# Block-sparse attention over gathered keys and values, and a feed-forward part without GpSimd, on one core

## The chip, the core and the metric

The kernel runs on one NeuronCore of a Trainium2 chip. The core has five engines that run at the same time, each with its own queue of instructions in a fixed order: TensorE (PE, matrix products; its weight loads are listed apart as PEld), VectorE (DVE), ScalarE (ACT), GpSimd (POOL) and SyncE (SP, which here only issues transfers). Engines wait for each other through semaphores. Data lie in SBUF, 128 partitions wide; matrix products land in PSUM, which has eight banks a partition; transfers between DRAM and SBUF, and within SBUF, are carried by 16 DMA engines. The metric is the device time of one execution in microseconds, the median of several.

## What is computed

Attention first, for 4 batches, 8 heads, 768 places and 64 numbers a head; then a feed-forward layer over the 3072 tokens with 512 inputs and 2048 hidden units.

```python
mask = np.abs(blk_i - blk_j) <= 1                       # blocks of 32 places, 24 of them
mask = mask | (blk_i == 0) | (blk_j == 0) | (blk_i == 23) | (blk_j == 23)
for qb in range(24):
    for kb in sampled_blocks[qb]:                       # three random blocks, the same for all heads
        mask[qb*32:(qb+1)*32, kb*32:(kb+1)*32] = True
attn = softmax(where(mask, q @ k.T / 8, -1e9))          # 1e-9 is added to the sum
x = (attn @ v), heads side by side                      # 3072 x 512
h = x @ w_in                                            # 3072 x 2048, weights given in float64
g = h * erf(log(1 + exp(h)))
out = g @ w_out                                         # 3072 x 512
```

So a query block in the middle (1 to 22) sees at most eight key blocks: its own and its two neighbours, blocks 0 and 23, and three random ones, some of which may coincide. Query blocks 0 and 23 see all 768 places.

## The kernel before

Attention goes head by head. A query tile has 128 queries of one head, and its scores are taken against all 768 keys, masked ones too. The mask is part of the product: 32 extra rows hold, for each query, a large negative number for each key block it must not see, and for each key the unit vector of its block (`mask_rows`, `spread`). In the first batch the product is taken in plain float32, four TensorE instructions a tile; later in two products of a rounded float32 and its remainder (`prep_head`, which also splits each head's values into a high and a low float16 half, L328 and L329). TensorE's line is L344.

A tile's softmax is: the row maximum (VectorE, L346), its scaling (L348), the exponential with the row sum (ScalarE, L350), a float16 copy (L356 on ScalarE or L358 on VectorE), the remainder in float16 (L360, mostly GpSimd), and one transposing transfer of both halves by SyncE (L362). Four tiles later `values` multiplies the transposed probabilities by the values: twelve products of 128 or 64 columns (L379, L380), and the quotient (L387 to L397). When a pair of heads is done, its outputs are split and transposed for the feed-forward part (L403 to L406).

The weights arrive as float64 bits, 32 pieces of 512 columns. VectorE takes each apart in three integer passes (L210 to L212); after the largest entry is known, each is scaled and split into two float16 halves in place (L290 to L297).

The feed-forward part works on 256 tokens and two hidden tiles of 128 at a time, a group of 512 columns; there are 96 groups. The first product has 24 matmuls of 256 columns (L460 to L462). Six passes of ScalarE (L464 to L475) and five of VectorE follow (L466, L473, L474, L476, L478), then the remainder of the float16 halves (L480), on GpSimd in three batches and on VectorE in the last. Three groups later the second product takes 12 matmuls of 512 columns (L492 to L494), in two halves.

The order of the work is set by a loop over query tiles: after each tile some steps of the weights and, with a credit for each batch, halves of feed-forward groups are issued. A planner places the instructions in the queues of the engines by a model of their times.

Of the kernel before, what the change touches and what calls it, by code (L numbers as in the profile page):

```python
# [10 lines left out]
F32R = mybir.dt.float32r  # L11
# [4 lines left out]
PSUM = bass.MemoryType.PSUM  # L16

P = 128
BLOCK = 32
NEG_BIG = float(2**33)  # /8 it exceeds the reference's 1e9  # L20
# [9 lines left out]
def sparse_attention_moe(ctx: ExitStack, tc: tile.TileContext, qT, kT, v, sampled, w_in, w_out, out):  # L30
    nc = tc.nc
# [4 lines left out]
    NQ = S // P  # query tiles, and key tiles, of a head  # L36
    NK = DM // P  # contraction tiles of the first product
    NF = DFF // P  # hidden tiles
    NR = sampled.shape[1]
    HB = min(512, S)  # L40
# [11 lines left out]
    st = ctx.enter_context(tc.tile_pool(name="st", bufs=4))  # L52
# [8 lines left out]
    # each batch's query tiles in two parts, head by head, so that the feed-forward part follows early  # L61
    hsegs = [(b, h, tuple(ts)) for b in range(B) for ts in (range(4), range(4, NQ)) for h in range(H)]
    raws = {}
    MR = slice(D, D + BLOCK)
    NATIVE = 2 * H  # parts of heads whose scores are taken in float32 as it is, while TensorE has time

    def stacked(n):
        """Places for two consecutive heads' queries and keys with the mask rows below them."""
        dt = F32 if n < NATIVE else F32R
        return [  # L70
            tuple(
                at.tile([D + BLOCK, S], dt, tag=f"{c}2", name=f"{c}2_{n}_{i}") for c in "qk"
            )
            for i in range(2)
        ]

    qk2 = {0: stacked(0)}

    def qk2_of(n):
        return qk2[0 if n < NATIVE else NATIVE][n % 2]  # L80

    def load_head(n):
        b, h, ts = hsegs[n]
        if n < NATIVE:
            q2, k2 = qk2_of(n)
            nc.sync.dma_start(q2[:D, : len(ts) * P], qT[b, h][:, ts[0] * P : (ts[-1] + 1) * P])
            nc.sync.dma_start(k2[:D], kT[b, h])
            return
        qraw = ld.tile([D, S], F32, tag="qraw", name=f"qraw_{n}", bufs=1)
        kraw = ld.tile([2 * D, S], F32, tag="kraw", name=f"kraw_{n}", bufs=1)  # L90
        nc.sync.dma_start(qraw[:, : len(ts) * P], qT[b, h][:, ts[0] * P : (ts[-1] + 1) * P])
        nc.sync.dma_start(kraw[:D], kT[b, h])
        nc.sync.dma_start(kraw[D:], kT[b, h])
        raws[b, h, ts] = (qraw, kraw)
# [3 lines left out]
    def load_v(b, h):  # L98
        vr = ld.tile([P, NQ, D], F32, tag="vraw", name=f"vraw_{b}_{h}", bufs=H)
        nc.sync.dma_start(vr, v[b][:, h])  # L100
        vraws[b, h] = vr

    load_head(0)

# [1 line left out]
    def pow2_scale(bound, tag, squared):  # L106
        """2^13 / 2^r and its inverse, on every partition, with 2^(r+1) above the largest entry
        of `bound`, or above its root."""
# [8 lines left out]
        zero = 63 if squared else 127  # what e is for r = 0  # L117
# [6 lines left out]

    vscale = {}

    vmax = {}

    def max_v(b, h):
        if b not in vmax:  # L130
            vmax[b] = st.tile([P, H], F32, tag="vmax", name=f"vmax_{b}", bufs=2)
        nc.vector.reduce_max(
            vmax[b][:, h : h + 1], vraws[b, h].rearrange("p k d -> p (k d)"), AX.X, apply_absolute_value=True
        )

    def scale_v(b):
        vscale[b] = pow2_scale(vmax.pop(b), f"v{b}", False)

# [1 line left out]

    unit = cp.tile([BLOCK, NB], F32, tag="unit", name="unit")
    nc.gpsimd.memset(unit, 1.0)
    nc.gpsimd.affine_select(unit, unit, [[1, NB]], ALU.is_equal, 0.0, base=0, channel_multiplier=-1)
    samp = at.tile([BLOCK, NB, NR, 2], I32, tag="pf", name="samp", bufs=3)
    nc.sync.dma_start(samp, sampled.bitcast(I32).rearrange("i (r w) -> i r w", w=2).partition_broadcast(BLOCK))
    hits = at.tile([BLOCK, 2, NB, NR], F32, tag="pf", name="hits", bufs=3)
    sampf, hit = hits[:, 0], hits[:, 1]
    nc.vector.tensor_copy(sampf, samp[:, :, :, 0])
    pidx = cp.tile([BLOCK, 1], F32, tag="pidx", name="pidx")
    nc.gpsimd.iota(pidx, [[0, 1]], base=0, channel_multiplier=1, allow_small_or_imprecise_dtypes=True)  # L150
    nc.vector.tensor_scalar(hit, sampf, pidx, None, ALU.is_equal)
    allow = cp.tile([BLOCK, NB], F32, tag="allow", name="allow")
    nc.vector.reduce_max(allow, hit, AX.X)
    # window |i-j| <= 1, key blocks 0 and NB-1, query blocks 0 and NB-1
    fixed = cp.tile([BLOCK, NB], F32, tag="fixed", name="fixed")
    nc.gpsimd.memset(fixed, 1.0)
    nc.gpsimd.affine_select(fixed, fixed, [[1, NB]], ALU.is_ge, 0.0, base=1, channel_multiplier=-1)
    nc.gpsimd.affine_select(fixed, fixed, [[-1, NB]], ALU.is_ge, 0.0, base=1, channel_multiplier=1)
    nc.gpsimd.affine_select(fixed, fixed, [[0, NB]], ALU.not_equal, 1.0, base=0, channel_multiplier=1)
    nc.gpsimd.affine_select(fixed, fixed, [[0, NB]], ALU.not_equal, 1.0, base=-(NB - 1), channel_multiplier=1)  # L160
    nc.gpsimd.memset(fixed[:, 0:1], 1.0)
    nc.gpsimd.memset(fixed[:, NB - 1 : NB], 1.0)
    nc.vector.tensor_tensor(allow, allow, fixed, ALU.max)
    bias = cp.tile([BLOCK, NB], F32, tag="bias", name="bias")
    nc.vector.tensor_scalar(bias, allow, -1.0, NEG_BIG, ALU.add, ALU.mult)

    def spread(rows, blocks):
        n = blocks.shape[1]
        nc.vector.tensor_copy(
            rows[MR, : n * BLOCK].rearrange("p (n c) -> p n c", c=BLOCK),  # L170
            blocks.unsqueeze(2).to_broadcast([BLOCK, n, BLOCK]),
        )

    masked = {}

    def mask_rows(n, ts):
        q2, k2 = qk2_of(n)
        key = (n >= NATIVE, n % 2)
        if key not in masked:
            spread(k2, unit)  # L180
# [410 lines left out]
```

## Time and profile before

| what | value |
|---|---|
| time, median of 3 runs | 1172.63 us (1172.04 to 1173.95) |
| span of the profiled execution | 1170.1 us; its own time outside the span is not listed, the median is 2.5 us above it |
| TensorE busy, mean granted clock | 910.7 us (78%), 0.876 |
| VectorE busy | 1045.3 us (89%) |
| ScalarE busy | 721.9 us (62%) |
| GpSimd busy | 662.0 us (57%) |
| moved by the DMA engines | 140.71 MB |

The page gives busy time by engine, a row of 40 slices, the chain of work that ended last, and groups of instructions. In a group's line stand the line of the kernel, the engine, the operation, what it writes and reads, shapes and count; behind the bar the busy time and the mean duration of one in ns; behind the second bar how long the engine was idle just before such instructions and what ended the wait. A TensorE instruction's duration includes the way through the array, so the distance between starts tells its rate. The granted clock is the share of full speed that TensorE was given.

### The profile page before, as it was taken

To read this page: it belongs to the slowest core of one execution; us is meant where nothing else is said; L and a number is where in the kernel's file an instruction comes from. 1 tells how busy PE (TensorE), PEld (TensorE's weight loads), DVE (VectorE), ACT (ScalarE), POOL (GpSimd) and SP (SyncE) were. 2 spreads that over 40 slices of the span, in tenths; PEclk is the share of its full clock that TensorE was granted. 3 is DMA by queue.
4 is the path that set the end of the run, shared out by engine and by line. 5 is a ranking of instruction groups with operands and counts; after the bars stand their busy time and mean duration, and the time that the engine had idled before them with its cause. 6 is when DMAs were issued, how large, how long until landed. Compare 5 with 4: busy or idle time off the path is not lost.

```text
span 1170.1 us, 18635 instructions
## 1 busy us (share of the span) xinstructions
PE 910.7 (78%) x6528; PEld 609.4 (52%) x6528; DVE 1045.3 (89%) x1672; ACT 721.9 (62%) x1389; POOL 662.0 (57%) x426
## 2 busy tenths in 40 slices
PE   4766666876888887776888888866988788889998
PEld 2433434543555654553665565544656555556664
DVE  6979976995999999996999999997998989997765
ACT  3557565763665766664666666654666765576775
POOL 1336674773767677685777667755666666741000
PEclk7566776897989989997988899897998989899999
DMA  9785966661665566763674567653744555451000
GB/s 331 137 240 125 216 128 138 129 118 34 133 131 115 115 147 137 138 141 72 121 157 98 115 129 165 127 130 75 132 99 101 122 111 119 96 93 34 20 18 19
DMA packets 354270, 140.71 MB, mean 120 GB/s; under 512 B 330976, under 2 KB 337152, under 8 KB 354176
## 3 DMA queue, kind: packets, MB, share of 16 engines
q1 hardware_dynamic: 350720, 133.23, 53.8%
q10 hardware_dynamic: 3456, 6.29, 1.6%
q8 instruction: 51, 0.84, 0.3%
q14 instruction: 43, 0.35, 0.1%
HBM read 51.40 MB, written 6.29 MB: 49 GB/s over the span
## 4 chain that ended last, share of the span: by engine, by line
DVE 58%; issue 13%; PE 10%; ACT 7%; DMA 3%; POOL 1%; SPq 0%; ACTq 0%; DVEq 0%; POOLq 0%
DVE mx L346 9%; DVE p L358 6%; DVE hs L476 6%; DVE x L466 5%; DVE s L474 5%; DVE s L473 4%; DVE vhl L329 4%; DVE g L478 2%; DVE q L321 2%; ACT pf L350 2%; DVE xf L397 2%; DMA pT<-p 2%; PE h L460 1%; PE h L461 1%; PE h L462 1%
## 5 line engine op out<-in xcount | busy, mean ns | idle before, releaser
L360 POOL TENSOR_TENSOR p<-pf,p 128x768 f16<-128x768 f32 x174 | 321.4, 1850 | 198.6 <-DVE p L358 62.5
L344 PE MATMUL s<-k,q 96*128 96x512 f32 (+3 forms) x768 | 265.4, 476 | 123.6 <-ACT pf L350 112.9
L350 ACT ACTIVATE pf<-s,nb 128x768 f32<-128x768 f32 x192 | 171.8, 895 | 147.1 <-DVE nb L348 119.7
L344 PEld LDWEIGHTS s<-k,q 96*128 96x128 f32 (+1 forms) x768 | 147.7, 225 | 203.7 <-ACT pf L350 129.5
L460 PE MATMUL h<-xT,wi 128*128 128x256 f16 x768 | 217.8, 284 | 14.5 <-DMA xT<-x 8.3
L462 PE MATMUL h<-xT,wi 128*128 128x256 f16 x768 | 216.9, 282 | 3.8 <-POOL wi L297 3.8
L461 PE MATMUL h<-xT,wi 128*128 128x256 f16 x768 | 217.4, 283 | 0.0
L379 PE MATMUL po<-vhl,pT 128*128 128x128 f16 x1152 | 143.7, 239 | 81.2 <-DVE y L392 41.0
L346 DVE TENSOR_REDUCE mx<-s 128x1 f32<-128x768 f32 x192 | 180.8, 943 | 6.8 <-PE s L344 6.7
L379 PEld LDWEIGHTS <-pT 128*128 128x128 f16 x1152 | 116.7, 110 | 112.8 <-issue 77.9
L494 PE MATMUL o<-wo,g 128*128 128x512 f16 x384 | 148.5, 396 | 21.8 <-POOL g L480 21.8
L492 PE MATMUL o<-wo,g 128*128 128x512 f16 x384 | 154.5, 402 | 10.5 <-DVE g L478 8.9
L493 PE MATMUL o<-wo,g 128*128 128x512 f16 x384 | 153.7, 400 | 0.0
L480 POOL TENSOR_TENSOR g<-hs,g 128x512 f16<-128x512 f32 x72 | 99.5, 1382 | 68.9 <-DVE g L478 53.8
L380 PE MATMUL po<-vhl,pT 128*128 128x64 f16 x1152 | 137.6, 209 | 0.0
L380 PEld LDWEIGHTS <-pT 128*128 128x128 f16 x1152 | 112.7, 106 | 12.3 <-issue 10.0
L475 ACT ACTIVATE s<-s 128x512 f32<-128x512 f32 x96 | 60.3, 628 | 93.2 <-DVE s L474 92.8
L474 DVE SCALAR_TENSOR_TENSOR s<-s,s 128x512 f32<-128x512 f32 x96 | 102.4, 1066 | 14.5 <-ACT s L472 13.6
L324 POOL TENSOR_TENSOR k<-kraw,k 64x768 fp32r<-64x768 f32 x48 | 103.4, 2154 | 18.5 <-DVE k L320 7.6
L467 ACT ACTIVATE x<-x 128x512 f32<-128x512 f32 x96 | 60.2, 627 | 86.8 <-DVE x L466 86.6
L358 DVE CAST p<-pf 128x768 f16<-128x768 f32 x124 | 104.0, 839 | 10.3 <-ACT pf L350 5.4
L476 DVE SCALAR_TENSOR_TENSOR hs<-s,hs 128x512 f32<-128x512 f32 x96 | 99.7, 1039 | 14.3 <-ACT s L475 14.1
(104 smaller groups left out, 1676.9 us busy)
## 6 DMA issues: line engine op xcount, KB each, us to landing
kraw<-in_kT_dram SPq DMA_DIRECT2D x96, 192.0 KB, 3.3
vraw<-in_v_dram SPq DMA_DIRECT2D x32, 192.0 KB, 2.8
wo<-in_w_out_dram SPq DMA_DIRECT2D x10, 512.0 KB, 5.1
wi<-in_w_in_dram SPq DMA_DIRECT2D x8, 512.0 KB, 6.1
wo<-in_w_in_dram SPq DMA_DIRECT2D x8, 512.0 KB, 9.3
k<-in_kT_dram SPq DMA_DIRECT2D x16, 192.0 KB, 3.3
pT<-p SPq DMA_TRANSPOSE x192, 3.7
qraw<-in_qT_dram SPq DMA_DIRECT2D x24, 128.0 KB, 3.0
```

The lines of the kernel that those rows point to most:

```text
L344: nc.tensor.matmul(s[:, c:e], lhs[:, qs], rhs[:, c:e], start=i == 0, stop=i == len(passes) - 1)
L346: nc.vector.reduce_max(mx, s[:, :S], AX.X)
L350: nc.scalar.activation(pf, s[:, :S], AF.Exp, bias=nb, scale=1.0 / math.sqrt(D), accum_out=sums[:, j : j + 1])
L358: nc.vector.tensor_copy(p2[:, 0], pf)
L360: eng.tensor_tensor(p2[:, 1], pf, p2[:, 0], ALU.subtract)
L379: nc.tensor.matmul(po[:, u, :], pT[:, k, :], vhl[:, k, :], start=k == 0, stop=False)
L380: nc.tensor.matmul(po[:, u, :D], pT[:, NQ + k, :], vhl[:, k, :D], start=False, stop=k == NQ - 1)
L460: nc.tensor.matmul(hj, hi, xa, start=kt == 0, stop=False)
L461: nc.tensor.matmul(hj, hi, xb, start=False, stop=False)
L462: nc.tensor.matmul(hj, lo, xa, start=False, stop=kt == NK - 1)
L474: nc.vector.scalar_tensor_tensor(s2, s1, C3, s2, ALU.add, ALU.mult)
L476: nc.vector.scalar_tensor_tensor(hs, s2, -1.0, hs, ALU.add, ALU.mult)
```

## The change

Attention no longer computes masked scores. The query blocks 1 to 20 of a batch form five tiles of four blocks; one unit is such a tile for four heads, 128 queries by 4 x 256 keys in two banks. For a block the 256 key places are: its own and two neighbouring blocks, read where they lie; three random blocks, copied within SBUF to a small buffer (`gather`), each by a SyncE transfer whose source is given by a register that SyncE reads from `sampled`; and blocks 0 and 23. There are six such buffers. Each block, head and piece is a product of its own, on an array of 64 rows and 32 columns, all in plain float32. Blocks 21 and 22 form a unit "e" for each four heads, and blocks 0 and 23, which see everything, a unit "f" for each two.

Values are split once for each batch and written to a table in DRAM with 32 rows of zeros at its end; a column of ones beside them gives the sums. GpSimd gathers the 256 rows of a block with two indirect transfers from a list of row numbers (`indices`, `gather_v`); a random block that coincides with another one is sent to the zero rows, so that it adds nothing to values or sums. The value products have 128 rows and 32 columns of the array and 64 or 65 streamed columns, four blocks in turn.

The weights are scaled and split in two passes instead of three, none on GpSimd. In the feed-forward part the remainder is always VectorE's; the second product follows two groups later instead of three. The feed-forward part may start when two query tiles of all heads are done, so a batch is released in three parts; it does not start before all weights are split. A quarter of the softmax remainders and the copies that reorder keys by blocks stay on GpSimd.

```diff
-NATIVE = 2 * H  # parts of heads whose scores are taken in float32 as it is, while TensorE has time
-    FF_LAG = 3  # groups between the two products
-    PV_LAG = 4  # query tiles between scores and values
+    KGS, VGS = 6, 8
+    FF_LAG = 2
+    PV_LAG = 2
...
+    def gather(b, i):
+        kg = at.tile([P, NR, HP, BLOCK], F32, tag="kg", name=f"kg_{b}_{i}", bufs=KGS)
+        for r in range(NR):
+            (load,), (n,) = nc.values_load_multi_w_load_instructions(
+                samp[0:1, i, r, 0:1], [mybir.EngineType.SP], min_val=0, max_val=NB - 1, ...)
+            tc.keep_in_program_order(load)
+            nc.sync.dma_start(
+                kg[:, r].rearrange("p a c -> p (a c)"),
+                kxs[b].rearrange("p n a c -> p n (a c)")[:, bass.ds(n, 1), :].rearrange("p n c -> p (n c)"),
+            )
...
+    def gather_v(b, quad, i):
+        vg = at.tile([P, 2, QW], F16, tag="vg", name=f"vg_{b}_{quad}_{i}", bufs=VGS)
+        if i < 0:
+            nc.sync.dma_start(vg, rows[:, -2 * i - 2 : -2 * i])
+        else:
+            for half in range(2):
+                nc.gpsimd.indirect_dma_start(out=vg[:, half], out_offset=None, in_=vtab[b, quad],
+                    in_offset=bass.IndirectOffsetOnAxis(ap=idx[:, half, i - 1 : i], axis=0))
...
-                if i % 2:
-                    nc.vector.tensor_scalar(w32, w32, s, None, ALU.mult)
-                else:
-                    nc.scalar.activation(w32, w32, AF.Copy, scale=s)
-                if i % 4:
-                    nc.scalar.activation(hi16, w32, AF.Copy)
-                else:
-                    nc.vector.tensor_copy(hi16, w32)
-                nc.gpsimd.tensor_tensor(lo16, w32, hi16, ALU.subtract)
+                nc.scalar.activation(hi16, w32, AF.Copy, scale=s)
+                nc.vector.scalar_tensor_tensor(lo16, w32, s, hi16, ALU.mult, ALU.subtract)
...
+    def softmax(s, groups, width, tag, u, place="pT"):
+        nc.vector.reduce_max(mx, s.rearrange("p (g w) -> p g w", w=width), AX.X)
+        nc.vector.tensor_scalar(nb, mx, -1.0 / math.sqrt(D), P_SHIFT * math.log(2.0), ALU.mult, ALU.add)
+        for g in range(groups):
+            nc.scalar.activation(pf[:, c], s[:, c], AF.Exp, bias=nb[:, g : g + 1], scale=1.0 / math.sqrt(D))
+        nc.scalar.activation(p3[:, :, 0], pf3, AF.Copy)
+        eng = nc.gpsimd if pick(u, 0.25) else nc.vector
+        eng.tensor_tensor(p3[:, :, 1], pf3, p3[:, :, 0], ALU.subtract)
+        nc.sync.dma_start_transpose(out=pT, in_=p2)
...
+    def key_columns(b, i, rows, pr):
+        return (
+            (0, 96, kx[rows, i - 1 : i + 2, pr, :]),
+            (96, 192, kg[rows, :, pr, :]),
+            (192, 256, kx[rows, 0 : NB : NB - 1, pr, :]),
+        )
...
+            for r in range(2):
+                pr = 2 * quad + r
+                for j in range(4):
+                    for a in range(2):
+                        rows, o = slice(a * D, a * D + D), slice(j * 32, j * 32 + 32)
+                        for c, e, keys in key_columns(b, 1 + 4 * t + j, rows, pr):
+                            nc.tensor.matmul(s4[o, a, r, c:e], qt[rows, pr, o], keys, start=True, stop=True)
...
+            for m in range(max(len(x) for x in todo)):
+                for j in range(4):
+                    if m < len(todo[j]):
+                        lhs, rhs = todo[j][m]
+                        nc.tensor.matmul(
+                            po[j * 32 : j * 32 + 32, hl, :w], lhs, rhs, start=m == 0, stop=m == len(todo[j]) - 1
+                        )
...
-        eng = nc.vector if b == B - 1 else nc.gpsimd
-        eng.tensor_tensor(g[:, 1], hs, g[:, 0], ALU.subtract)
+        nc.vector.tensor_tensor(g[:, 1], hs, g[:, 0], ALU.subtract)
...
+    units += [("m", b, t, quad) for t in range(MT) for quad in range(2)]
+    units += [("e", b, 0), ("f", b, 0), ("f", b, 1), ("f", b, 2), ("e", b, 1), ("f", b, 3)]
...
+    ready = []
+    for b in range(B):
+        for n in (4, 8, per):
+            ready.append((b * per + n + PV_LAG, 2 * NGR * (len(ready) + 1)))
+    for m in range(total):
+        if m >= PV_LAG:
+            finished(units[m - PV_LAG])
+        if m < len(units):
+            scores(units[m], m)
+            gathers()
+            behind(m)
+        if m < 6:
+            for _ in range(5):
+                next(wgen, None)
+        may = max([g for u, g in ready if u <= m], default=0)
+        if may:
+            if done == 0:
+                for _ in wgen:
+                    pass
+            left = min([u for u, g in ready if u > m], default=total + 4) - m
+            for _ in range(-(-(may - done) // left)):
+                next(ff, None)
+                done += 1
```

More of the change, by code (lines that the diff above doesn't have):

```diff
@@ L160, in sparse_attention_moe @@
[L160 to L172, printed above, removed]
@@ L228, in load_raw @@
         for raw in parts:
-            nc.sync.dma_start(raw, rows[:, c : c + raw.shape[1]])
+            eng = nc.scalar if key == "i" and i < 8 else nc.sync
+            eng.dma_start(raw, rows[:, c : c + raw.shape[1]])
             c += raw.shape[1]
-    def halves(i):
-        return [
-            mo.tile([P, 512], I32, tag=tag, name=f"raw_{i}_{u}", bufs=bufs)
-            for u, (tag, bufs) in enumerate(lent[2 * (i - 8) : 2 * (i - 7)])
-        ]
     def raw_place(key, i):
@@ L253, in weights @@
         places = {}
-        order = [("i", i) for i in range(16)] + [("o", i) for i in range(16)]
+        order = [("i", i) for i in range(16)] + [("o", i) for i in (*range(8), *range(12, 16), *range(8, 12))]
         loaded = decoded = 0
         def free(key, i):
-            if key == "i" or 8 <= i < 13:
+            if key == "i" or i >= 12:
                 return True
-            return decoded >= min(10 + i, 16) if i < 8 else decoded >= 24 and (i < 15 or "i" in split)
+            return decoded >= min(10 + i, 16) if i < 8 else decoded >= 24
         def load_until(m):
@@ L514, in feed_forward @@
                 yield
-    ready = []
-    n_units = n_halves = 0
-    for b, h, ts in hsegs:
-        n_units += len(ts)
-        if h == H - 1:
-            n_halves += len(ts) // CT * NGR * CT
-            ready.append((n_units + PV_LAG + 1, n_halves))
-    wgen, ff = weights(), feed_forward()
-    next(wgen)
-    for h in range(H):
-        load_v(0, h)
-    load_head(1)
-    for h in range(H):
-        max_v(0, h)
-    scale_v(0)
-    done = 0
-    credit = w_credit = 0.0
-    for m, _ in enumerate(attention()):
-        w_credit += 1.6
-        while w_credit >= 1.0:
-            next(wgen, None)
-            w_credit -= 1.0
-        may = max([g for u, g in ready if u <= m + 1], default=0)
-        credit = min(credit + (0.84, 0.68, 1.1, 1.2)[min(m // (NQ * H), B - 1)], may - done) if may else 0.0
-        while credit >= 1.0:
-            while done == 0 and "raw" not in split:
-                next(wgen)
-            if done == CT * FF_LAG:
+    units = []
@@ new lines, in finished @@
+    def finished(unit):
+        nonlocal vfree
+        if unit[0] == "m":
+            values(*unit[1:])
+            vfree += 4
+        elif unit[0] == "f" and unit[2] % 2 == 1:
+            values(unit[1], MT, unit[2] // 2)
+            vfree += 5
+    wgen, ff = weights(), feed_forward()
+    for pr in range(HP):
+        load_k(0, pr)
+    have_k.add(0)
+    load_q(0, 0)
+    load_v(0, 0)
+    next(wgen)
+    max_v(0, 0)
+    load_v(0, 1)
+    max_v(0, 1)
+    for half in range(2):
+        split_v(0, 1, half)
@@ new lines, in sparse_attention_moe @@
+    load_v(0, 0)
+    for half in range(2):
+        split_v(0, 0, half)
+    have_v.add(0)
+    gathers()
+    ready = []
+    for b in range(B):
+        for n in (4, 8, per):
+            ready.append((b * per + n + PV_LAG, 2 * NGR * (len(ready) + 1)))
+    total = len(units) + PV_LAG
+    done = 0
+    for m in range(total):
[3 more added lines that the diff above has]
+            scores(units[m], m)
+            if units[m][0] == "m" and units[m][3] == 1:
+                kfree += 4
+            elif units[m][0] == "e" and units[m][2] == 1:
+                kfree += 2
+            gathers()
+            behind(m)
[5 more added lines that the diff above has]
+            if done == 0:
+                while "raw" not in split:
+                    next(wgen)
```

517 lines of the change are left out of this document (301 added, 216 removed).

## The prediction

> **What bounds the kernel now.** I read the page first: the busy table, the granted clock by slice, and the chain of waits by engine.
>
> ```profile
> span 1170.1 us, 18635 instructions
> PE 910.7 (78%) x6528; PEld 609.4 (52%) x6528; DVE 1045.3 (89%) x1672; ACT 721.9 (62%) x1389; POOL 662.0 (57%) x426
> ...
> PEclk7566776897989989997988899897998989899999
> ...
> DVE 58%; issue 13%; PE 10%; ACT 7%; DMA 3%; POOL 1%; SPq 0%; ACTq 0%; DVEq 0%; POOLq 0%
> ```
>
> VectorE is busy 89% of the span and carries 58% of the chain: it is the bound. TensorE is second, at a clock that sags early. Next I asked why VectorE is so full, with the groups by shape, once for the whole run and once for the last 70 us, where GpSimd does nothing.
>
> ```profile
> L476 DVE SCALAR_TENSOR_TENSOR hs<-s,hs 128x512 f32<-128x512 f32 x96 | 99.7, 1039 | 14.3 <-ACT s L475 14.1
> L466 DVE TENSOR_SCALAR x<-hs,isg 128x512 f32<-128x512 f32 x96 | 89.4, 931 | 2.9 <-ACT hs L464 2.9
> L478 DVE CAST g<-hs 128x512 f16<-128x512 f32 x96 | 61.2, 638 | 1.1
> L360 POOL TENSOR_TENSOR p<-pf,p 128x768 f16<-128x768 f32 x174 | 321.4, 1850 | 198.6 <-DVE p L358 62.5 <-ACT p L356 44.5 <-DVE rinv L387 33.0
> ```
>
> ```profile
> L476 DVE SCALAR_TENSOR_TENSOR hs<-s,hs 128x512 f32<-128x512 f32 x13 | 9.0, 692 | 7.1 <-ACT s L475 7.0
> L480 DVE TENSOR_TENSOR g<-hs,g 128x512 f16<-128x512 f32 x13 | 9.0, 692 | 0.4
> ...
> L474 DVE SCALAR_TENSOR_TENSOR s<-s,s 128x512 f32<-128x512 f32 x12 | 8.3, 692 | 6.3 <-ACT s L472 6.0
> L473 DVE SCALAR_TENSOR_TENSOR s<-x 128x512 f32<-128x512 f32 x12 | 8.3, 690 | 3.3 <-ACT x L468 3.3
> ...
> L466 DVE TENSOR_SCALAR x<-hs,isg 128x512 f32<-128x512 f32 x12 | 5.8, 485 | 2.6 <-ACT hs L464 2.6
> L478 DVE CAST g<-hs 128x512 f16<-128x512 f32 x13 | 5.5, 422 | 0.4
> ```
>
> The same instruction takes 931 ns over the run and 485 ns at the end (L466), 1039 against 692 (L476), 638 against 422 (L478). What is missing at the end is GpSimd's work. So a good part of VectorE's 1045 us is VectorE held up while GpSimd works, and the change takes most of that work away.
>
> **The change, engine by engine.** *VectorE.* The feed-forward keeps 96 groups. One group, undisturbed, is 0.485 + 0.690 + 0.692 + 0.692 + 0.422 + 0.692 = 3.67 us, the low half now VectorE's own; 96 of them are 353 us. The weights:
>
> ```profile
> L211 DVE SCALAR_TENSOR_TENSOR mag<-wi,mag 128x512 int32<-128x512 int32 x9 | 6.2, 685 | 0.1
> L210 DVE TENSOR_SCALAR mag<-wi 128x512 int32<-128x512 int32 x9 | 5.9, 656 | 0.1
> ...
> L212 DVE SCALAR_TENSOR_TENSOR wi<-wi,mag 128x512 int32<-128x512 int32 x8 | 6.8, 851 | 0.1
> ```
>
> Decoding is 32 x 2.19 = 70 us; the new split in one pass is 32 x 0.69 = 22 us. Attention falls from 192 softmax tiles of 768 columns to 40 of 1024, 8 of 512 and 16 of 768.
>
> ```profile
> L346 DVE TENSOR_REDUCE mx<-s 128x1 f32<-128x768 f32 x192 | 180.8, 943 | 6.8 <-PE s L344 6.7
> L360 DVE TENSOR_TENSOR p<-pf,p 128x768 f16<-128x768 f32 x18 | 19.1, 1059 | 4.3 <-ACT p L356 3.5 <-issue 0.8
> L392 DVE TENSOR_TENSOR y<-po,vlo 128x256 f32<-128x256 f32 x32 | 13.1, 410 | 0.0
> ```
>
> Scaled by columns, a unit of 1024 is a maximum of 1.26 us, three quarters of a subtraction of 1.41, one scaling of 0.41 and some 0.5 of small ones: 3.2 us, so 40 x 3.2 = 128; the smaller units are 8 x 1.6 + 16 x 2.0 = 45; the queries' split, the values' split and maxima some 60. Sum 353 + 92 + 128 + 45 + 60 = 678, and with 30 for the 16 subtractions left on GpSimd about 710 us, against 1045. VectorE ceases to be the bound.
>
> *ScalarE.* Six passes of a group, 32 squares and 32 halves, and four exponentials (0.37 each at 256 columns, L390 below) and one copy of 1024 (836 x 1024/768 = 1.11) a unit:
>
> ```profile
> L356 ACT ACTIVATE p<-pf 128x768 f16<-128x768 f32 x68 | 56.8, 836 | 4.0 <-issue 3.5
> L468 ACT ACTIVATE x<-x 128x512 f32<-128x512 f32 x96 | 59.9, 624 | 1.6
> L390 ACT ACTIVATE vlo<-po 128x256 f32<-128x256 f32 x32 | 11.8, 367 | 0.0
> ```
>
> 96 x 3.7 + 32 x 1.4 + 40 x 2.6 + some 90 = 594 us. Not a bound.
>
> *GpSimd* gives up its subtractions and gets 352 gathers of value rows. No row shows such a gather. The nearest are a cross-partition maximum of 0.38 us, and 1.85 us for L360 above:
>
> ```profile
> L112 POOL PARTITION_ALL_REDUCE allm_v<-top_v x4 | 1.5, 377 | 25.5 <-issue 25.5
> ```
>
> That is 134 to 651 us, beside everything else, two units ahead of its reader; I take 1.2 us, 420 in all.
>
> *TensorE.* Here work is added. The feed-forward's 3456 matmuls stay; scores become 48 products a unit on arrays of 64 rows by 32 columns, in plain float32, values 96 products a unit on 128 by 32. The timeline of TensorE has the nearest rows, at full clock unless said:
>
> ```profile
> 170.00 1.56 PE L344 MATMUL s<-k,q 96*128 96x512 f32 x4 [0.65 <-ACT pf L350]
> 171.40 0.22 PE L379 MATMUL po<-vhl,pT 128*128 128x128 f16 x1
> 171.46 0.19 PE L380 MATMUL po<-vhl,pT 128*128 128x64 f16 x1
> 171.48 0.22 PE L379 MATMUL po<-vhl,pT 128*128 128x128 f16 x1
> ```
>
> ```profile
> 195.38 2.69 PE L344 MATMUL s<-k,q 96*128 96x512 f32 x4
> 197.90 0.27 PE L460 MATMUL h<-xT,wi 128*128 128x256 f16 x1
> 198.01 0.27 PE L461 MATMUL h<-xT,wi 128*128 128x256 f16 x1
> ```
>
> ```profile
> 642.95 0.38 PE L492 MATMUL o<-wo,g 128*128 128x512 f16 x1
> 643.17 0.38 PE L493 MATMUL o<-wo,g 128*128 128x512 f16 x1
> ```
>
> Starts, not durations, give the rate. A plain float32 product of 768 columns is four instructions (two passes) and takes 171.40 - 170.00 = 1.40 us, less about 0.1 for its first weight load: 1.69 ns a column. (At 195.38 it takes 2.52: half clock.) A float16 pair of 128 and 64 columns takes 171.48 - 171.40 = 0.08 us, so one of 65 columns 0.08 x 65/192, some 0.028; one of 256 takes 0.11, one of 512 0.22. So the feed-forward is 2304 x 0.11 + 1152 x 0.216 = 502 us. Scores of one unit are 16 places of 256 columns, 4096 columns x 1.69 = 6.9 us; values 96 x 0.028 = 2.7 us; the edge blocks 16 x 1.3 + 8 x 1.7 + 8 x 192 x 0.028 = 77. Attention is 40 x 9.6 + 77 = 461 us. TensorE's sum is 963 us at full clock, above its 911 busy us of before, part of which ran at half clock; it becomes the bound.
>
> A small array is used alone here, if its neighbours wait: the code gives one place's three key pieces, six instructions, before the next place. Of each six, the last (64 columns in one pass, 0.054 us) can run beside the next place's first. I take that off: 16 x 0.054 = 0.9 us a unit, 35 in all, 928.
>
> *The start.* Nothing of the feed-forward begins until all 32 pieces of weights are split and four units' values are out. VectorE has by then 92 for weights, seven units x 3.2 = 22, and 20 for values and indices, 134 us, after some 8 us of loads: 142. The whole start is paid with TensorE nearly idle: it does 7 x 6 + 5 x 2.7 = 56 us of its 928 there.
>
> *SyncE.* Each block's random keys are three copies, each after a register read that no row prices. A plain copy holds the queue 0.47 us and lands 3.2 us after it, a transposing one holds it 1.43:
>
> ```profile
> L92 SPq DMA_DIRECT2D kraw<-in_kT_dram x48: 465/466/1632, 182.9 to 1017.2; - x48
> ...
> DMA to landing us min/median/max: 2.9/3.2/4.7
> ```
>
> ```profile
> L362 SPq DMA_TRANSPOSE pT<-p x192: 1273/1433/5971, 20.8 to 1060.1; - x192
> ```
>
> Six key places let one pair of units run and hold half the next, so six copies must be issued after a pair's scores and before the next pair's. At 0.5 us each that is 3 + 3.2 = 6 us; at 2.9 (a transpose's hold and as much again for the read) 20 us. TensorE covers it with values and two to four halves of a feed-forward group, 2.7 + 2 or 4 x 2.6 = 8 to 13 us. So 0, or at worst 10 us in each of some 18 pairs, 180. I take 1 us a copy: 9 us, hidden. Behind the waiting copy stand softmax's transposes, whose readers come two units later.
>
> **The sum.** 142 + (928 - 56) + 10 for the last group's chain = 1024 with TensorE never idle. It will be idle at times, since its queue is in order:
>
> ```profile
> 900.00:1000.00 100.00, 83.10 (x663) 58.77 (x660) 93.69 (x142) 65.72 (x125) 62.30 (x39) 0.95 0.54 109
> 1100.00:1170.00 70.00, 64.78 (x430) 41.67 (x428) 44.59 (x77) 46.62 (x76) 0.00 (x0) 1.00 0.04 16
> ```
>
> VectorE as the bound was 94% busy; TensorE at the end 93%, with nothing but feed-forward to fill gaps. I take 95%: 872/0.95 = 918, and a span of 142 + 918 + 10 = 1070. The span before is 1170.1 and the median 1172.6, 2.5 us more, so about 1073 us. Its own range, with 90% to 100%, the clock at 0.95 and SyncE half hidden, is 1020 to 1160.
>
> **Rivals.** *Places side by side* (0.16). Score products of neighbouring places run at once, down to the pace of one product in 0.028 us: 96 x 0.028 = 2.7 us a unit in place of 6. After the start that is 33 x 3.3/0.95 = 115 us less, a time of about 958. For it: each place writes other rows or another bank. Against: six instructions of one place come in a row. The Trainium skill, TensorE: Matmul & The Clock Gate, Part 3, has products on different places of the array starting about 4 ns apart, and sixteen of them 10.6 times as fast; no run here shows it yet.
>
> *Weights in the open* (0.14), the slower side. Every small product loads its own weights, 192 loads a unit. In the rows before, a load hides under the product ahead:
>
> ```profile
> L344 PEld LDWEIGHTS s<-k,q 96*128 96x128 f32 x480 | 96.7, 234 | 108.9 <-ACT pf L350 55.8 <-issue 38.7 <-DVE q L169 6.4
> ```
>
> A quarter of its 234 ns (32 of 128 columns) is 58 ns against products of 54 to 81 ns. If a load can't run beside a product of the same place, the 33 units after the start cost 33 x 96 x 0.058/0.95 = 193 us more: 1266. It is slower than before from 30 ns a product on. For it: no row shows a partial array. Against: the rows' spacing has no trace of loads. The Trainium skill, TensorEngine Tiling (Array Packing), Restrictions, says that column tiling switches Fast Weight Load off, which speaks the same way; it says nothing of float32.
>
> *The clock* (0.08). A unit's attention is 9 us of small products. If they don't hold the clock up, it falls to a half within them:
>
> ```profile
> 30.00:40.00 10.00, 8.53 (x26) 4.15 (x25) 9.90 (x18) 4.61 (x11) 3.18 (x2) 0.50 0.61 107
> ```
>
> TensorE at 85% busy has half clock here. Half of 9 us twice as slow, and the feed-forward's first 2 us too, 6.5 us in 58 steps: 1450. Against: from the seventh slice on (200 us), where feed-forward lies between, the page's slices are mostly at 0.8 or above.
>
> *GpSimd still holds VectorE up* (its gathers instead of its subtractions; the change then misses its aim). By L476, L466 and L478 the held-up group takes 1.63 times as long: 96 x 6.0 = 574 in place of 353, a sum of 931, at 94% 990: still under TensorE. No new time.
>
> **How the numbers follow.** Forecast 0.62, the rivals 0.16, 0.14, 0.08. About 0.2% (2.3 us) is what a measurement tells from no change. Of the forecast's own cases nearly all are faster, 0.02 within and 0.02 slower: faster 0.58 + 0.16 = 0.74, same 0.02, slower 0.24. The range 910 to 1290 takes in the first two rivals with some room and SyncE's 180 us, and leaves out the clock and the far ends, some 0.15.
>
> **What would show it.** VectorE near 700 us and L466's successor near 485 ns; TensorE the fullest engine after 145 us, at 0.95 clock; scores of one unit 6 to 7 us from first to last start, values 2.7; the first feed-forward product after 130 us. Wrong if the scores' places start within some ns of each other, if loads stand between them, if TensorE waits for keys from SyncE, or if the clock sinks in the middle.

## The result, and the profile after

The changed kernel takes 1288.08 us (median of 4 runs, 1285.24 to 1289.90), the kernel before 1173.29 beside it: a ratio of 1.0974, 95% interval 1.0955 to 1.0992. It is slower by 9.7%, where 1073 us and faster was forecast. The profiled execution took 1289.44 us with a span of 1287.6.

The page of the changed kernel: busy times, TensorE's granted clock by slice, and two rows of the DMA queues (packets, MB, share of 16 engines).

```profile
span 1287.6 us, 30573 instructions
...
PE 930.6 (72%) x12928; PEld 634.4 (49%) x12928; DVE 647.0 (50%) x1190; ACT 575.2 (45%) x1009; POOL 413.0 (32%) x415
...
PEclk9999557878887876878997887889998788879999
...
q0 software_dynamic: 16896, 46.88, 14.2%
...
q8 instruction: 101, 1.65, 0.5%
```

VectorE fell from 1045.3 to 647.0 us, as the change meant it to, and no engine took its place: the fullest, TensorE, is at 72%. The time is made of waits. The start first, in stretches of 50 us (busy time and instructions of PE, PEld, DVE, ACT, POOL; clock, DMA share, GB/s):

```profile
50.00:100.00 50.00, 7.01 (x83) 6.10 (x83) 34.59 (x72) 15.72 (x40) 14.95 (x16) 1.00 0.64 204
100.00:150.00 50.00, 18.20 (x419) 14.45 (x418) 11.35 (x25) 6.89 (x13) 21.96 (x27) 0.79 0.56 146
150.00:200.00 50.00, 23.64 (x446) 19.13 (x446) 28.20 (x52) 24.85 (x43) 24.14 (x23) 0.60 0.59 147
```

From 100 to 200 us no engine is busy more than 56% of the time (VectorE, 28.20 of 50). The first feed-forward product is one of these (first and last start in the row):

```profile
L533 PE MATMUL h<-xT,wi x768: 269/273/421, 201.0 to 1272.8; 128*128 128x256 f16 x192
```

What the engines wait for, over the whole run (us in total, times, longest; "issue" is time in which the engine waited for nothing that the profile shows):

```profile
POOL vg L265 <- PE po L483: 391.3, 38, 18.0
PEld s_m L427 <- issue: 223.5, 221, 49.5
...
PE s_m L427 <- issue: 112.0, 163, 2.9
...
PE s_m L427 <- DMA kg<-kx: 68.1, 11, 49.1
```

The products of the scores (`s_m`, L427, the PE rows) stand still for 112.0 us with nothing that holds them, 163 times. The row of their weight loads (PEld) is not to be added: 105.8 of its 223.5 us are these same pauses, and the rest lies beside other waits of the products (its longest, 49.5, beside the 49.1 for keys) or beside running products. The wait for the copied keys (`kg<-kx`) is only 68.1 us, and most of that is one wait at the start. What the pauses look like is seen in one unit, the scores alone, in steps of 2 us (columns as above, with only PE, PEld, DVE and ACT); the last row is a unit without them:

```profile
524.80:526.80 2.00, 2.00 (x51) 2.00 (x52) 0.00 (x0) 0.00 (x0) 1.00 0.43 121
526.80:528.80 2.00, 0.97 (x12) 0.49 (x10) 0.00 (x0) 0.00 (x0) 1.00 0.44 112
528.80:530.80 2.00, 1.06 (x12) 0.73 (x12) 0.00 (x0) 0.00 (x0) 1.00 0.56 141
530.80:532.80 2.00, 1.29 (x11) 0.78 (x9) 0.00 (x0) 0.00 (x0) 0.63 0.92 200
532.80:534.80 2.00, 1.09 (x8) 0.72 (x8) 0.00 (x0) 0.00 (x0) 0.50 0.29 96
...
657.30:661.00 3.70, 3.55 (x96) 3.39 (x96) 0.00 (x0) 0.00 (x0) 1.00 0.23 58
```

The undisturbed unit issues its 96 product instructions (48 products, two each) and 96 loads in 3.6 us. The other starts at the same pace, 103 instructions in 2 us, and then gets 24 to 16 in 2 us, until it is done after 13 us; on the way the granted clock falls from 1.00 to 0.50. In the same stretch GpSimd issues row gathers, two in 2 us, which wait for the values just ahead of these scores (`POOL vg <- PE po`; the columns here are PE, with the last of those values, and POOL):

```profile
524.80:526.80 2.00, 0.07 (x9) 1.34 (x2) 1.00 0.43 121
526.80:528.80 2.00, 0.00 (x0) 1.70 (x2) 1.00 0.44 112
```

Below, TensorE is called starved of instructions in such pauses. That is a reading: the profile shows only that it stands still and names nothing that it waits for.

### The profile page after: what moved, and what is told of

Read it like the earlier page. It is cut to its first block, busy times and chain, and to the rows that moved or that the text cites. A ratio compares the mean times of both kernels' runs of the same rounds, so it can differ in the third digit from the quotient of the medians.

```text
span 1287.6 us, 30573 instructions
## 1 busy us (share of the span) xinstructions
PE 930.6 (72%) x12928; PEld 634.4 (49%) x12928; DVE 647.0 (50%) x1190; ACT 575.2 (45%) x1009; POOL 413.0 (32%) x415
## 3 DMA queue, kind: packets, MB, share of 16 engines
q8 instruction: 101, 1.65, 0.5%
## 5 line engine op out<-in xcount | busy, mean ns | idle before, releaser
L265 POOL DMA_INDIRECT vg<-vtab,idx x352 | 361.9, 1028 | 491.4 <-PE po L483 391.3
L427 PE MATMUL s_m<-kx,qt 64*32 64x96 f32 (+1 forms) x2560 | 225.1, 265 | 120.6 <-issue 72.1
L427 PE MATMUL s_m<-kg,qt 64*32 64x96 f32 x1280 | 183.1, 279 | 108.5 <-DMA kg<-kx 68.1
L427 PEld LDWEIGHTS s_m<-kx,qt 64*32 64x32 f32 x2560 | 174.3, 120 | 149.4 <-issue 97.9
L427 PEld LDWEIGHTS s_m<-kg,qt 64*32 64x32 f32 x1280 | 142.3, 125 | 126.2 <-issue 125.7
L388 ACT ACTIVATE pf_m<-s_m,nb_m 128x256 f32<-128x256 f32 x160 | 62.5, 475 | 212.3 <-DVE nb_m L384 196.8
L537 ACT ACTIVATE hs<-h 128x512 f32<-128x512 f32 x96 | 57.3, 596 | 155.9 <-PE h L535 84.9
L539 DVE TENSOR_SCALAR x<-hs,isg 128x512 f32<-128x512 f32 x96 | 55.4, 577 | 129.0 <-ACT hs L537 117.1
L534 PEld LDWEIGHTS <-wi 128*128 128x128 f16 x768 | 81.5, 106 | 46.7 <-issue 29.4
L533 PEld LDWEIGHTS <-wi 128*128 128x128 f16 x768 | 81.3, 106 | 39.4 <-issue 18.9
L546 DVE SCALAR_TENSOR_TENSOR s<-x 128x512 f32<-128x512 f32 x96 | 69.8, 727 | 58.1 <-ACT x L541 50.1
L535 PEld LDWEIGHTS <-wi 128*128 128x128 f16 x768 | 82.2, 107 | 23.5 <-issue 7.7
L549 DVE SCALAR_TENSOR_TENSOR hs<-s,hs 128x512 f32<-128x512 f32 x96 | 66.3, 691 | 41.4 <-ACT s L548 33.8
```

The source lines that it names most:

```text
L265: nc.gpsimd.indirect_dma_start(out=vg[:, half], out_offset=None, in_=vtab[b, quad], in_offset=bass.IndirectOffsetOnAxis(ap=idx[:, half, i ...
L388: nc.scalar.activation(pf[:, c], s[:, c], AF.Exp, bias=nb[:, g : g + 1], scale=1.0 / math.sqrt(D))
L427: nc.tensor.matmul(s4[o, a, r, c:e], qt[rows, pr, o], keys, start=True, stop=True)
L533: nc.tensor.matmul(hj, hi, xa, start=kt == 0, stop=False)
L534: nc.tensor.matmul(hj, hi, xb, start=False, stop=False)
L535: nc.tensor.matmul(hj, lo, xa, start=False, stop=kt == NK - 1)
```

## The experiments

Times are single runs unless an interval is given; the kernel before took 1172.6 to 1175.4 us beside each group.

**One suspect taken away at a time.** Theory A: the gathers' traffic on GpSimd's queue starves TensorE of instructions. B: it is the list of rows. C (in this group): the late key copies alone.

```diff
 e1: -nc.gpsimd.indirect_dma_start(out=vg[:, half], in_=vtab[b, quad], in_offset=...idx...)
     +nc.gpsimd.dma_start(vg[:, half], vtab[b, quad][half * P : half * P + P])
 e2: +vgs[b, quad, i] = vfix; return      # one constant place, no gather
 e6: +kgs[b, i] = kfix; return            # one constant place, no copy
 e3: -finished(units[m - PV_LAG]); scores(units[m], m)
     +scores(units[m], m); finished(units[m - PV_LAG])
```

e1 leaves out which rows the values read, e2 the middle blocks' values, e6 the sampled keys; e3 computes everything. (e2, and e7, e10 and e12 below, have one place fewer for rows or keys, since the constant one takes its room.)

> Only the way of the value transfers changes: each half of a block's 256 value rows is read by a plain transfer of the same 128 x 1040 bytes from fixed rows of the table, still issued by GpSimd (the values read are not the block's, so the output differs). Theory A: while the gathers move data on GpSimd's queue, TensorE gets its instructions too slowly (154 ns from one score instruction to the next in such times, 43 ns in others, in the changed kernel's trace). If it is the traffic of GpSimd's queue, whatever its row list, this stays at 1270 to 1300 us with scores still at 7 to 15 us a unit. Theory B: the row list (single rows picked one by one) is the cause: scores fall to about 3.5 us and the time by some 150 us to about 1130. Theory C: scores wait for their keys from SyncE alone: no change, 1280 to 1295.

> The value gathers are left out: all blocks read one place filled with ones (the output is not the attention's). Theory A (the gathers' traffic starves TensorE of instructions): score units fall from a mean of about 9 us to 3.5 to 5, the clock rises from 0.855 to above 0.9, and the time falls by 150 to 250 us, to 1040 to 1130. Theory C (late keys alone): 1250 to 1290, with the same waits on the key copies.

> The random keys' copies and their register reads are left out: all blocks read one place filled with 0.1 (the scores of the random places are not the attention's). Theory C (keys late on SyncE's queue bound it): the start shortens by 30 to 60 us and score units lose their waits, time 1100 to 1150. Theory A: score units stay at 7 to 13 us wherever the value gathers move data; only the waits on the copies (68 us by the table of waits, most of them in the start) go: 1200 to 1250.

> One exchange of order: in each step the scores of the new unit are issued ahead of the values of the unit two before. The value gathers, which wait for those values to free their places, then run beside the feed-forward's large products and not beside the scores' small ones. Theory A: score units fall to 3.5 to 5 us and the time by 80 to 170 us, to 1120 to 1210. Theory C: no change or slightly faster, 1260 to 1290.

Measured: 1035.05, 992.54, 981.00 and 1027.45 us. Each gave back some 250 to 307 us, which can't all be true of one sum; e1 spoke for B, though 95 us under its 1130, and e2, e6 and e3 came out under A's ranges, e6 under C's as well. I first took this for causes that need each other, and looked for what the key copies add.

**What in the copies?** Theory D: their traffic. E: their lateness. F: SyncE's register loads. With these, one part of the change alone (e5), and scores first with a quicker start (e9).

```diff
 e5 (on the kernel before): -eng = nc.vector if b == B - 1 else nc.gpsimd
                            +eng = nc.vector
 e7: -kgs[b, i] = kg              +kgs[b, i] = kfix      # copied, not read
 e8: -kxs[b][:, bass.ds(n, 1)]    +kxs[b][:, 5 + r]      # no register load
 e9 (on e3): -nc.gpsimd.tensor_copy(kxs...)   +nc.vector.tensor_copy(kxs...)  # first batch
             +gathers()                       # keys, ahead of the values' tables
```

> One part of the change alone, on the kernel before: the feed-forward's low half is always VectorE's, as in the changed kernel. The 72 subtractions leave GpSimd (99.5 us there) and cost VectorE 72 x 0.69 to 1.04 = 50 to 75 us; in return VectorE is held up less. Theory of the prediction (VectorE is held up for as long as GpSimd works, by about half of that time): about 45 us come back, so 1165 to 1200 us, no gain by itself. Rival (the feed-forward's speed in the changed kernel comes from this edit): under 1130 us.

> The changed kernel with all its copies of key places on SyncE's queue, register loads included, but nobody reads them: the scores of the 32-row blocks take one constant place of 0.1 (the sampled keys are left out of the scores). It keeps the copies' traffic and takes away that TensorE waits for them. Theory D (TensorE's instructions run dry when the copies and the value rows move during its scores: it is the traffic of both): 1200 to 1290 us, over 100 ns from start to start in the scores while rows move. Theory E (it is the lateness of the keys, which puts scores, values and rows on top of each other): 975 to 1040 us, under 40 ns. Theory F (the register loads on SyncE disturb): as D.

> The changed kernel with the same copies of key places, read by the scores as before, but from fixed places (blocks 5, 6 and 7) with no register load: which keys are copied is left out. A copy takes SyncE 0.49 us in place of 0.94, so six blocks' copies 8.8 us in place of 17. Theory D (traffic of copies and rows): 1200 to 1290 us. Theory E (late keys): the copies stay behind the softmax's transfer, but land 8 us earlier: 1080 to 1220 us. Theory F (register loads): 975 to 1050 us.

> The order scores before values, as in the run before, and a quicker start: the first batch's keys are laid out by VectorE instead of GpSimd, and the first six blocks' key copies are issued ahead of the values' tables. In the run before, the first copies were issued at 80 us and the first feed-forward product came at 181 us. If the keys hold up the start: the first product comes at 140 to 160 us and the time is 985 to 1010 us. If the weights and the values' tables hold it up: 1015 to 1035 us, first product after 170 us.

Measured: e5 1160.23 against 1175.35 (a single run each), e7 1297.47, e8 1251.52, e9 1111.91. E and F fall: without the wait, and without the register loads, the time hardly moves. e9 misses both its ranges. In e5 the groups show what the prediction had reasoned from, on a smaller scale:

```profile
L480 DVE TENSOR_TENSOR g<-hs,g 128x512 f16<-128x512 f32 x96 | 81.2, 846 | 0.9
L466 DVE TENSOR_SCALAR x<-hs,isg 128x512 f32<-128x512 f32 x96 | 77.9, 812 | 5.3 <-ACT hs L464 5.3
```

Taking 72 subtractions from GpSimd brings L466 from 931 to 812 ns; what VectorE gains pays for the work it takes over (1049.1 us busy against 1045.3), and the time ends 5 us under the theory's range.

**Traffic, place or program?** Theory D as before; G: where tables and programs lie; H: SyncE's instructions, whatever they move.

```diff
 e10 (on e7): +for r in range(NR if b == 0 else 0):      # copies in the first batch only
 e11: +pad = dr.tile([3000, 1024], F32, ...)             # tables of value rows lie 12 MB further
 e12 (on e7): kg[:1, r]...[:, :1] <- kx[:1, n, :1]       # copies of one number
 e13: scores; half of the feed-forward's share; values and gathers; the other half
```

> As the run with unread copies (1297 us), but only the first batch's key places are copied; the second batch has no copies at all. In the run with all copies, scores of the second batch's last units still took 13 us each though no copy had run for 20 us. Theory D (the copies' traffic, at the time): the second batch's scores take 3.3 to 5 us a unit, the first's 9 to 15, about 1130 to 1190 us. Theory G (nothing that happens at the time, but where the program's tables, places and instructions lie): both batches alike, 1250 to 1300 or 960 to 1010 us.

> The changed kernel with 12 MB of unused device memory allocated ahead of the tables of value rows, so that the tables lie elsewhere; nothing else is different but one write of 1 KB. Theories D and H: 1275 to 1300 us, no change. Theory G (where things lie in device memory): a change of over 60 us, to either side, most likely down to 1000 to 1150 us.

> As the run with unread copies, but each of the 264 copies moves one number instead of 64 KB; register loads and issues on SyncE stay as they are, and the sampled keys are left out of the scores. Theory D (the copies' traffic): 970 to 1020 us, scores at 20 to 30 ns from start to start. Theory H (SyncE's loads and issues, whatever they move): 1240 to 1300 us. Theory G: either of the two.

> The whole change in another order: scores first, then half of the feed-forward's share, then values and their row gathers, then the other half. No burst of short products is longer than one unit's 192 instructions (scores or values) before feed-forward follows, whose instructions are consumed at some 14 to 18 a microsecond. In all theories TensorE's stalls in scores and values shrink against the run with scores first (40 and 54 us): 960 to 1010 us. If it is 1020 or more, bursts following each other were not what was left there.

Measured: 1261.41, 1279.59, 1315.32, 1234.91. D falls with e12 (no traffic, no gain), H with e10: its last copy is issued at 222.4 us, and in its third and fourth batch, after 640 us, the products of the scores still pause 156 times for 72.0 us. G as tried in e11 changes nothing. In e13 the gathers, released in mid feed-forward, reach into the next scores, whose products pause 144 times for 113.9 us: the order meant as a cure has as many as the changed kernel. And e12 differs from e6, 334 us faster, by no more than register reads and 264 transfers of one number. What also differed was the chip: the first group had run on one, these on others, and the changed kernel had not run beside any.

**The same kernels with the changed one beside them.** From here on theory C is: the chip decides.

> The changed kernel itself, as a control beside the next three on one chip. The four runs so far that were fast (no key copies, scores first, plain transfers, no value gathers) came from one chip, on which the changed kernel had not run, and all later ones from others. Theory C (the chip, not the edits, decides whether TensorE is starved while the row lists move): where this is near 1288, the three others are starved too; where it is near 1000 to 1050, they are as fast as before. Theory E/G (the edits): 1288 here and the others fast.

> No key copies at all (one constant key place of 0.1 in the scores of the 32-row blocks; the sampled keys are left out), a second time: 981 us before, though three kernels with hardly more than its register loads took 1261 to 1315. Theory C: 1230 to 1310 us where the control is near 1288. Theory G: near 981 again.

> Scores before values, the whole computation, a second time and timed: 1027 us before. Theory C: 1080 to 1250 us where the control is near 1288 (its own sister with earlier key copies took 1112 on another chip, the one with values apart 1235). Theory G: 1020 to 1035.

> The value rows by GpSimd's plain transfers from fixed rows (which rows are gathered is left out), a second time: 1035 us before. Theory C with the queue as such as the cause: 1200 to 1300 us where the control is near 1288. Theory B (the row list is the cause): near 1035 again on any chip.

Measured on this one chip: changed kernel 1268.71 (ratio to before 1.0804, 1.0725 to 1.0884), no key copies 1253.69, scores first 1126.14 (0.9614, 0.9566 to 0.9663), plain transfers 1033.33. The kernel without key copies, the same file, is 273 us slower than on the first chip. One unit's scores in its two traces, first on the first chip, then on this one, both with two or three row gathers issued in each 2 us:

```profile
414.00:416.00 2.00, 2.00 (x60) 2.00 (x62) 0.00 (x0) 0.00 (x0) 1.00 0.71 197
416.00:418.00 2.00, 1.46 (x43) 1.29 (x36) 0.00 (x0) 0.00 (x0) 1.00 0.56 157
```

```profile
479.60:481.60 2.00, 2.00 (x52) 2.00 (x53) 0.00 (x0) 0.00 (x0) 1.00 0.44 126
481.60:483.60 2.00, 1.12 (x12) 0.64 (x10) 0.00 (x0) 0.00 (x0) 1.00 0.44 113
483.60:485.60 2.00, 1.51 (x13) 0.91 (x12) 0.00 (x0) 0.00 (x0) 0.69 0.34 100
485.60:487.60 2.00, 1.97 (x15) 1.79 (x14) 0.00 (x0) 0.00 (x0) 0.50 0.46 125
```

And the pauses of the scores' products over the run, again first chip, then this one:

```profile
PE s_m L432 <- issue: 6.5, 9, 1.7
```

```profile
PE s_m L432 <- issue: 130.2, 275, 1.6
```

So the first group's gains of e6, and part of those of e3, were the chip's, or those of something else that differed between the two groups and is not on record; e6 has a single run on each. On a chip that has the pauses, the order is worth 143 us; key copies show 15, no more than the two runs of the changed kernel lie apart there (1261.37 and 1276.04). e2 was not run on such a chip. The plain transfers took 1035.05 and 1033.33 on the two chips: without a list of rows there are hardly any pauses on either. The changed kernel's pauses on this chip, then the waits with plain transfers:

```profile
PE s_m L427 <- issue: 98.2, 153, 4.6
```

```profile
PE s_m L422 <- DMA kg<-kx: 89.6, 18, 45.6
...
PE s_m L422 <- issue: 6.9, 6, 2.5
```

6 pauses in place of 153. With values and feed-forward, TensorE's products pause without a named cause for 175.5 us in the changed kernel and 8.6 here, where the two spans are 228 us apart; the mean granted clock is 0.874 and 0.932. It is not that the plain transfers come more thinly. One unit's scores with them, then the transfers in the same stretch (PE, POOL):

```profile
425.50:429.20 3.70, 3.55 (x96) 3.39 (x96) 0.00 (x0) 0.00 (x0) 1.00 0.64 180
```

```profile
425.50:429.20 3.70, 0.14 (x18) 3.25 (x7) 1.00 0.64 180
```

GpSimd is busy with such transfers, each of 128 rows, for 3.25 of 3.7 us, all queues together move 180 GB/s, and the 96 products keep their pace. In the changed kernel's unit above it was two gathers in 2 us, at 121 GB/s.

**The right rows, without a list.** The plain transfers had read fixed, neighbouring rows, and had held GpSimd for 189.4 us against 361.9. The last two kernels fetch each block's own rows by five plain transfers on GpSimd's queue; they compute everything.

```diff
 e21: -nc.gpsimd.indirect_dma_start(... idx[:, half, i - 1 : i] ...)
      +nc.gpsimd.dma_start(vg[0:96, 0], tab[(i - 1) * 32 : (i + 2) * 32])
      +nc.gpsimd.dma_start(vg[64:128, 1], tab[...blocks 0 and NB - 1])
      +for p0, half in ((96, 0), (0, 1), (32, 1)):
      +    n = <register read on GpSimd of idx[p0, half, i - 1]>
      +    nc.gpsimd.dma_start(vg[p0 : p0 + 32, half], tab[bass.ds(n, 32)])
 e22: the same on e3
```

> The whole computation in the changed kernel's order, with no row list: each block's 256 value rows come by five plain transfers on GpSimd's queue, three of them from a row number read into a register. That is some 880 transfers and 528 register reads on GpSimd in place of 352 gathers; by the plain transfer's 0.54 us and SyncE's 0.27 us a read, some 3.5 us a block, 620 us in all, or 14 us for a unit's four blocks. Theory B (the row list starves TensorE): scores at under 50 ns from start to start while GpSimd's transfers run, 1035 to 1110 us, the upper part if GpSimd's issues now keep the values waiting. Rival (any steady traffic on GpSimd's queue starves TensorE, and the run with plain transfers had too little of it): 1200 us or more.

> The same with scores before values. Theory B: the order no longer matters much, within 30 us of the run before it, and under the 1126 us that row lists with scores first took. Rival: as with row lists, some 100 us under the run before it.

Measured: 1245.21 (1.0591, 1.0555 to 1.0627) and 1254.46 (1.0700, 1.0661 to 1.0739). e21's time misses B's range and lies in its rival's; e22's is within 30 us of it, as B said, but not under 1126. The waits speak against the rival: first those of e21's values and scores, then GpSimd's groups.

```profile
PE po L497 <- DMA vg<-vtab: 27.3, 6, 13.0
...
PE s_m L441 <- issue: 13.8, 6, 4.1
```

```profile
L284 POOL DMA_DIRECT2D vg<-vtab x528 | 267.7, 508 | 313.6 <-issue 287.1 <-DMA vg<-vtab 25.3 <-DVE x L553 0.4
L272 POOL DMA_DIRECT2D vg<-vtab x176 | 125.2, 711 | 9.4 <-issue 5.3 <-DMA vg<-vtab 4.0
L267 POOL DMA_DIRECT2D vg<-vtab x176 | 94.5, 537 | 114.5 <-PE po L497 102.4 <-DMA vtab<-vn 5.0 <-issue 1.9
```

6 pauses, as with plain transfers, though GpSimd now issues 880 and more, and the order no longer matters (9 us). But these two ran on a fifth chip, where no kernel with lists ran beside them, and the first chip had hardly any pauses even with lists. So that the right rows come without pauses on every chip is not shown; what stands against mere traffic is the unit of plain transfers above. Whether it is the list itself or the scatter of the rows it names, no run separates.

The time has gone elsewhere. GpSimd spends 267.7 + 287.1 + 125.2 + 94.5 = 775 us on the pieces, 287.1 of it standing before transfers that need a register; 620 had been expected. Its wait for free places, 393.5 us with plain transfers, is down to 102.4. TensorE is seen waiting for rows only six times, 27.3 us; how the rest of the 212 us over the plain transfers comes about is not shown.

The best whole computation is scores first: 1126.14 us, faster than the kernel before by 3.9% and than the changed one by 11%, on a chip with the pauses.

## Why the prediction was wrong, step by step

*VectorE.* Right. 647.0 us against "about 710"; and the feed-forward's instructions lost most of their hold-up. The groups of the changed kernel by shape, with the gathers:

```profile
L265 POOL DMA_INDIRECT vg<-vtab,idx x352 | 361.9, 1028 | 491.4 <-PE po L483 391.3 <-issue 92.3 <-DMA vtab<-vn 4.6
...
L549 DVE SCALAR_TENSOR_TENSOR hs<-s,hs 128x512 f32<-128x512 f32 x96 | 66.3, 691 | 41.4 <-ACT s L548 33.8 <-issue 6.6
...
L539 DVE TENSOR_SCALAR x<-hs,isg 128x512 f32<-128x512 f32 x96 | 55.4, 577 | 129.0 <-ACT hs L537 117.1 <-issue 9.7 <-ACT pf_f L388 1.6
```

L539 takes 577 ns against 485 forecast and 931 before, L549 691 against 692. *ScalarE* is at 575.2 against 594. *GpSimd's gathers* are 1028 ns against 1.2 us. The rival that GpSimd still holds VectorE up did not happen.

*TensorE's sum of 928 us.* Wrong by its two estimates: an undisturbed unit's scores take 3.6 us, not 6, and values are some 1 us, not 2.7 (90 products in 0.91 us):

```profile
523.97 0.91 PE L483 MATMUL po<-vg,pT_m 128*32 128x65 f16 x90
524.80 0.35 PE L427 MATMUL s_m<-kx,qt 64*32 64x96 f32 x2
524.99 0.24 PE L427 MATMUL s_m<-kg,qt 64*32 64x96 f32 x1
525.00 0.27 PE L427 MATMUL s_m<-kx,qt 64*32 64x96 f32 x1
```

The rival "places side by side" had the array nearly right (2.7 us for the scores): 40 units cost some 40 x 4.6 = 184 us instead of 348, so TensorE needs 502 + 184 + at most 77 = 763 us. With plain transfers it is still the fullest engine, but busy only 796.3 of 1031.6 us. "Weights in the open" came near in time (1266) by luck and is wrong: 96 loads run beside 96 product instructions in the 3.6 us.

*The start, 142 us.* Measured 201.0. The sum counted VectorE alone. The pauses are the larger part of what it missed: on one chip the first feed-forward product comes at 198.9 us in the changed kernel and at 160.2 with plain transfers. SyncE's order is another: the first key copies stand behind the values' tables, which wait for the values' split, and without any copies the product comes at 177.6 there. e9, on a further chip, issued the first copies at 54.8 us instead of some 80, and its first product still came at 192.4.

*SyncE.* 1 us a copy was right after the start, "hidden" only mostly. SyncE's timeline, at the start and later:

```profile
85.04 28.48 SPq L251 DMA_DIRECT2D kg<-kx  x18
...
491.00 1.85 SPq L399 DMA_TRANSPOSE pT_m<-p_m  x1
494.08 12.88 SPq L251 DMA_DIRECT2D kg<-kx  x12
```

The first 18 copies take 28.48 us and begin at 85.04. Later 12 take 12.88, but they stand behind the softmax's transpose; the prediction had it the other way round ("Behind the waiting copy stand softmax's transposes"). The products' wait for keys is 68.1 us in the changed kernel and 89.6 with plain transfers, of which 49.1 and 45.6 are the one wait of the start.

*95% for TensorE.* The step that failed, and that decided. It took for granted that TensorE, once it has its data, keeps going; from 200 us on it is busy 81% of the time (880.8 of 1087.6 us). It stands still while GpSimd's row lists move: on one chip, 98.2 us of pauses in the scores' products against 6.9 with plain transfers, 175.5 against 8.6 in all products, and 1269 against 1033 us. No term and no rival had it. "The clock" was a rival at 1450: the clock does fall, to 0.50, but in the pauses and after them; the undisturbed unit above runs at 1.00.

The 1288 us lie just inside the range of 910 to 1290, by luck: that end was drawn for loads in the open and for SyncE's copies, not for this. Without the lists the kernel takes 1033 us, 4% under the forecast. That is no proof of the sum: TensorE was put some 165 us too high, the start (first product at 160.2 us there) too low, and the waits for keys were not counted.

## What to carry to other kernels

A kernel of many small products draws instructions far faster than one of large products (100 instructions in 2 us here, against some 28 of the feed-forward by the prediction's rates, 72 in 5.2 us), so ask of every transfer beside it whether instructions still arrive; the sign in the profile is an engine that pauses with no semaphore named, in the waits as "issue". Count it on the products alone: the weight loads' row tells the same pauses again, and other waits with them. Run the kernel under study beside its variants on the same chip: four variants without that control looked like four causes, and for one of them nearly all of the gain was the chip. A gather by list can be replaced by plain transfers, but price each register read and each issue on the queue that takes them: here that replacement (1245 us) did not beat the lists with scores first (1126), though on another chip.

## What the runs showed of the hardware

- While lists of rows (352 gathers of 128 rows) move, TensorE issues some 8 instructions a microsecond in a dense stretch (the last 89 of a unit's 192 in 11.0 us), where 50 were issued before. Plain transfers of the same size on the same queue and chip do not do this: 6 pauses of the scores' products against 153. In more pieces, on another chip, there were 6 as well.
- It differs by chip, as far as single runs tell: the scores' products of the same file paused 9 times on one chip and 275 times on another. The kernel before varies by 0.24% over the five chips (1172.55 to 1175.35). Whether the changed kernel itself is quick on the first chip was not run.
- The instruction queue moved 101 packets, 1.65 MB, for 2 x 12928 products and loads: 256 instructions to a packet. The Trainium skill, Advanced Engine Details and Errata, ISA Cache, has lines of 16 KB for 256 instructions; the trace agrees with the size. These packets take no longer where TensorE pauses: by the traces' packet records 1.04 us in the median in the changed kernel, 1.02 with plain transfers on the same chip, 1.06 on the first chip without key copies. So how a list of rows slows TensorE, and why by chip, stays open: moving the tables did nothing either.
- Values on four places of 32 columns start some 10 ns apart (90 in 0.91 us), scores on two row places some 37 ns (96 in 3.55 us), with the loads hidden.
- A register-addressed copy holds SyncE for about 1.07 us (12 in 12.88); GpSimd stands some 0.54 us ahead of each of the 528 transfers that need a register, which themselves take 0.51 (287.1 and 267.7 us in all).
